# Streaming V past stationary softmax probabilities, with the row sum as a 65th column, in an attention-plus-experts kernel

## The chip, the cores and the metric

The kernel runs on one NeuronCore of a Trainium2 chip. The metric is the device time of the whole program in microseconds (us). Most figures are medians. A ratio is the mean time of one kernel's fast runs over the mean of the fast runs of the kernel before in the same rounds, so it isn't quite the ratio of the medians that stand beside it. Below, PE is TensorE, PEld its weight loads, DVE is VectorE, ACT is ScalarE.

## The reference, cut to what matters

Four batches of eight heads, 768 positions, head size 64. Three heads are full causal, five see a window of 64 and four sink positions. The attention result is the input of eight experts, weighted by a Sinkhorn-normalised router.

```python
scores = scale * np.matmul(q, k.transpose(0, 1, 3, 2))          # (4, 8, 768, 768)
scores = np.where(mask[None], scores, -1e9)
a = np.exp(scores - scores.max(-1, keepdims=True))
a = a / (a.sum(-1, keepdims=True) + 1e-9)
x = heads_side_by_side(np.matmul(a, v))                          # (3072, 512)
P = np.exp(x @ w_gate - (x @ w_gate).max())                      # router
for _ in range(8):
    P /= P.sum(1, keepdims=True) + 1e-9
    P /= P.sum(0, keepdims=True) + 1e-9
    P *= N / E
for e in range(8):
    out += P[:, e:e+1] * (np.maximum(x @ w1[e], 0) @ w2[e])
```

## The kernel before

Scores are computed transposed: keys on the partitions, 256 queries on the free axis. ACT takes the exponential into `PT`, DVE multiplies by masks. A unit (b, g, u) is 256 queries of four heads, done as two head pairs a = 0, 1. The product with V and the denominators are two sets of matmuls that stream the same `PT`:

```python
def gen_pv(b, g, u, a, PT, scale):
    if a == 0:
        accs[b, g, u] = [psA.tile([128, 512], F32, tag="pv", bufs=2, ...) for i in range(2)]
    pv, den = accs[b, g, u]
    for i, (kj, far, lo, hi, off) in enumerate(todo):
        cols = slice(256 * a + lo, 256 * a + hi)
        for hh in range(2):                      # two heads, on partitions 0-63 and 64-127
            nc.tensor.matmul(out=pv[64 * hh:64 * hh + 64, cols],
                             lhsT=(vf if far else vt)[:, h, kj, :],
                             rhs=PT[:, hh, off:off + hi - lo], ...)
        for hh in range(2):                      # row sums, 64 times over
            nc.tensor.matmul(out=den[64 * hh:64 * hh + 64, cols],
                             lhsT=onesf[:, h, min(kj, 1), :] if far else ones16,
                             rhs=PT[:, hh, off:off + hi - lo], ...)
        yield
    if a == 1:                                   # 1 / den as exp(-ln(den)), then one scaling
        nc.scalar.activation(out=rc, in_=den, func=AF.Ln, ...)
        nc.scalar.activation(out=rc, in_=rc, func=AF.Exp, scale=-1.0)
        scale.append(lambda: nc.vector.tensor_tensor(out=xT[u][:, :, c0:c0 + 256], in0=pv, in1=rc, op=ALU.mult))
```

Attention runs in 48 rounds. A round computes scores, their exponentials and masks, and in some rounds the products that have become ready. Between them PE gets "fillers": pieces of the first expert's layers for blocks of `x` that are finished (a layer-1 piece is one unit, a layer-2 piece two, 96 units in all). What is left runs between the Sinkhorn steps. In attention the kernel holds eight PSUM tiles of 128x512 f32, called banks here: four for scores, two for `pv` and `den`, two (tag `mo`) shared by fillers, preparing transposes of Q and K, and router logits.

The softmax here doesn't subtract the row's maximum and nothing guards it: scores larger than these inputs give would overflow.

## Time and profile before

| | us |
|---|---|
| median, 5 runs | 733.41 (732.26 to 733.88) |
| attention with fillers, to the first column-sum matmul | 184.8 |
| Sinkhorn loop with the rest of the fillers | 20.3 |
| experts 1 to 7 | 525 |

The busy time of each engine in these three stretches of the kernel before (columns: stretch, its length, then busy us and instruction counts by engine, granted PE clock, DMA share and GB/s):

```profile
core 0: us, PE busy (x) PEld busy (x) DVE busy (x) ACT busy (x) POOL busy (x), PEclk, DMA share, GB/s
0.00:184.80 184.80, 169.57 (x2258) 111.27 (x2258) 107.81 (x231) 126.95 (x180) 39.73 (x51) 1.00 0.74 78
184.80:205.10 20.30, 19.70 (x136) 13.01 (x137) 14.87 (x43) 9.18 (x16) 1.32 (x2) 1.00 0.12 20
205.10:730.00 524.90, 516.48 (x4682) 457.34 (x4681) 448.12 (x845) 292.47 (x600) 110.26 (x131) 1.00 0.57 97
```

PE looks 92% busy in attention (169.57 of 184.80 us), but the records of matmuls overlap: one of 256 columns lasts 273 ns, and the next pair starts after 109. As what a matmul takes from the array I count the distance to the next start. The timeline of PE before shows it (start, length, line, shape, count):

```profile
100.79 0.28 PE L296 MATMUL pv<-PT,vf 128*64 128x256 f16 x2
100.89 0.28 PE L303 MATMUL pv<-PT,onesf 128*64 128x256 f16 x2
101.00 0.28 PE L296 MATMUL pv<-PT,vf 128*64 128x256 f16 x2
101.11 0.28 PE L303 MATMUL pv<-PT,onesf 128*64 128x256 f16 x2
...
101.44 0.22 PE L296 MATMUL pv<-PT,v 128*64 128x128 f16 x2
101.50 0.22 PE L303 MATMUL pv<-PT,ones 128*64 128x128 f16 x1
```

A pair of 256-column matmuls, one head in each half of the array, takes 0.11 us and not 0.28; a pair of 128 columns takes 0.06. The rows alternate between product (L296) and denominator (L303): half of this time goes into row sums.

For every matmul I took the distance to the next start, capped at the spacing that the trace shows where nothing waits: 216 ns at 512 columns, 109 at 256, 56 at 128, 25 at 8. (In the count the cap is the straight line through the first three, and never below 25 ns.) These "occupied" times sum to 142.4 of 184.8 us in attention, 37.8 us of it for product and denominator. The other 42.4 us are waits, switches of tile mode (89 to 96 ns where the records show one without a wait: after a 256-column matmul, for one, the next start comes after 205 ns in place of 109 where the mode changes from 128x128 to 64x128; 165 switches by program order), a slow start (512-column matmuls 427 ns apart in the first 5 us) and a few lost records. In the expert phase the same count gives 513.5 of 525 us, so nothing is to be had there.

The instructions behind the accumulation, from the groups of the attention stretch (busy us, mean ns, then idle time before them and its releaser):

```profile
L314 DVE TENSOR_TENSOR xT<-pv,rc 128x512 f16<-128x512 f32 x24 | 16.5, 689 | 6.8 <-ACT rc L312 6.7
L312 ACT ACTIVATE rc<-rc 128x512 f32<-128x512 f32 x24 | 15.2, 635 | 0.5
L311 ACT ACTIVATE rc<-pv 128x512 f32<-128x512 f32 x24 | 14.5, 604 | 10.5 <-PE pv L303 10.5
```

Ln and Exp cost ACT 29.7 us, and each unit's two accumulators stay taken until they and the scaling are done.

### The profile page before, as it was taken

The page shows a single profiled execution, that of the slowest core. Times are in us where ns is not written, and L with a number is a line of the kernel's source. Part 1 is how long each engine was busy: PE and PEld are TensorE (multiplying, and loading weights), DVE is VectorE, ACT ScalarE, POOL GpSimd, SP SyncE. Part 2 cuts the span into 40 slices and gives each one's busy share as a digit, 9 for nine tenths or more (in the row PEclk, how much of TensorE's full clock was granted, in tenths as well). Part 3 has the DMA queues.
Part 4 walks back from the last instruction along what each step waited for, and adds up shares of the span by engine and source line. Part 5 has one row for each costly group of instructions (what it writes and reads, how often), then busy time and mean ns, then how long its engine had stood idle before and what let it go on. Part 6 is the DMA issues. An engine that isn't in the chain of part 4 may idle for free.

```text
span 730.4 us, 17366 instructions
## 1 busy us (share of the span) xinstructions
PE 705.7 (97%) x7072; PEld 581.6 (80%) x7072; DVE 570.8 (78%) x1118; ACT 428.6 (59%) x795; POOL 151.3 (21%) x183
## 2 busy tenths in 40 slices
PE   7898999999999999999999999999999999999996
PEld 3566576766758888888888888888888888888884
DVE  5646565564788998888788888888889888977787
ACT  5666777777478555555555555555555555555550
POOL 6303131000001213121312131213121312121210
PEclk9999999999999999999999999999999999999999
DMA  9999575300063428742864386438743874345785
GB/s 178 180 165 74 58 58 47 31 2 2 1 116 57 75 45 135 113 82 48 138 110 79 52 136 111 76 57 132 114 74 59 123 124 73 59 71 107 149 157 126
DMA packets 84224, 65.62 MB, mean 90 GB/s; under 512 B 48304, under 2 KB 64688, under 8 KB 84144
## 3 DMA queue, kind: packets, MB, share of 16 engines
q0 software_dynamic: 74976, 57.17, 55.0%
q1 hardware_dynamic: 7536, 6.30, 3.8%
q8 instruction: 55, 0.90, 0.5%
q10 hardware_dynamic: 1632, 1.05, 0.5%
q14 instruction: 25, 0.20, 0.1%
HBM read 52.45 MB, written 6.29 MB: 80 GB/s over the span
## 4 chain that ended last, share of the span: by engine, by line
PE 67%; DVE 1%; issue 0%; ACT 0%; DVEq 0%
PE l1y L707 19%; PE l2y L776 19%; PE l2w L776 10%; PE l1w L707 10%; PE l2z L776 5%; PE l1z L707 5%; DVE acc L793 1%; DVE S L644 0%; ACT R L716 0%; DVEq L887 0%; ACT add L790 0%
## 5 line engine op out<-in xcount | busy, mean ns | idle before, releaser
L798 POOL DMA_DIRECT2D acc<-add x120 | 101.5, 845 | 381.6 <-ACT add L790 346.9
L716 ACT ACTIVATE R<-l1y 128x512 f32<-128x512 f32 x164 | 98.7, 602 | 127.8 <-PE l1y L707 92.8
L776 PEld LDWEIGHTS <-S 128*128 128x128 f16 x1344 | 131.1, 98 | 17.1 <-DVE S L644 1.2
L707 PEld LDWEIGHTS <-S 128*128 128x128 f16 x1312 | 128.3, 98 | 17.1 <-issue 2.1
L793 DVE SCALAR_TENSOR_TENSOR acc<-l2y,Pne,acc 128x256 f32<-128x256 f32 x256 | 111.2, 476 | 29.9 <-PE l2y L776 29.8
L776 PEld LDWEIGHTS <-hT 128*128 128x128 f16 x1008 | 98.6, 98 | 12.0 <-issue 0.6
L707 PEld LDWEIGHTS <-w 128*128 128x128 f16 x984 | 96.3, 98 | 11.9 <-issue 0.6
L707 PE MATMUL l1y<-T,S 128*128 128x256 f16 x656 | 98.4, 273 | 1.4 <-ACT R L716 1.4
L448 ACT ACTIVATE PT<-sc 128x1024 f16<-128x1024 f32 (+1 forms) x96 | 83.7, 920 | 26.4 <-PE sc L439 25.1
L776 PE MATMUL l2y<-T,S 128*128 128x256 f16 x672 | 87.1, 273 | 0.0
L790 ACT ACTIVATE add<-l2w,Pne 128x256 f32<-128x256 f32 x80 | 33.7, 473 | 66.1 <-PE l2w L776 62.3
L644 DVE TENSOR_TENSOR S<-hT 128x1024 f16<-128x1024 f16 x84 | 57.6, 685 | 17.0 <-ACT hT L746 14.6
L722 DVE CUSTOM_DVE_ANT_0 hT<-l1z,R 128x512 f16<-128x512 f32 x82 | 56.2, 685 | 7.4 <-ACT R L716 7.3
L722 DVE CUSTOM_DVE_ANT_0 hT<-l1w,R 128x512 f16<-128x512 f32 x82 | 56.1, 685 | 4.3 <-PE l1w L707 0.4
L722 DVE CUSTOM_DVE_ANT_0 hT<-l1y,R 128x512 f16<-128x512 f32 x82 | 55.7, 679 | 0.1
L346 PE MATMUL l<-xT,w 128*128 128x256 f16 x384 | 49.4, 273 | 3.2 <-DVE xT L314 1.4
L746 ACT ACTIVATE hT<-l1y 128x512 f16<-128x512 f32 x82 | 49.0, 597 | 4.2 <-PE l1y L707 2.8
L716 ACT ACTIVATE R<-l1w 128x512 f32<-128x512 f32 x82 | 49.4, 603 | 0.0
L707 PE MATMUL l1z<-xT,w 128*128 128x256 f16 x328 | 49.4, 273 | 0.0
L707 PE MATMUL l1w<-T,S 128*128 128x256 f16 x328 | 49.4, 273 | 0.0
L707 PE MATMUL l1w<-xT,S 128*128 128x256 f16 x328 | 49.4, 273 | 0.0
L707 PE MATMUL l1y<-T,w 128*128 128x256 f16 x328 | 49.2, 272 | 0.1
(104 smaller groups left out, 1111.6 us busy)
## 6 DMA issues: line engine op xcount, KB each, us to landing
acc<-add POOLq DMA_DIRECT2D x120, 256.0 KB, 3.3
w<-in_moe_w_dram POOLq DMA_DIRECT2D x16, 1024.0 KB, 10.7
out_dram<-acc SPq DMA_DIRECT2D x44, 128.0 KB, 2.8
k<-in_k_dram POOLq DMA_DIRECT2D x11, 256.0 KB, 5.6
q<-in_q_dram POOLq DMA_DIRECT2D x11, 256.0 KB, 7.0
v<-in_v_dram POOLq DMA_DIRECT2D x12, 192.0 KB, 8.0
acc<-in_v_dram POOLq DMA_DIRECT2D x3, 256.0 KB, 7.5
acc<-in_q_dram ACTq DMA_DIRECT2D x2, 256.0 KB, 5.3
```

What stands on the lines that cost most here:

```text
L346: nc.tensor.matmul(out=l1[:, ts(fb % 2, 256)], lhsT=w1[:, dc, ts(fb, 128)], rhs=xT[dc // 2][:, dc % 2, c0:c0 + 256], start=(dc == 0), stop ...
L448: nc.scalar.activation(out=PT[:, :, c0:c0 + width], in_=sc[:, :, 0:width], func=AF.Exp, bias=0.0, scale=SCALE,)
L644: nc.vector.tensor_tensor(out=out_, in0=a_, in1=b_, op=op)
L707: nc.tensor.matmul(out=banks[g, bank][:, f, :], lhsT=lefts1[e][k - 1][:, dc, ts(2 * g + f, 128)], rhs=rights1[c][k - 1][:, dc, :], start=( ...
L716: nc.scalar.activation(out=R[name], in_=banks[g, bank], func=AF.Copy, bias=0.0, scale=1.0)
L722: nc.vector._custom_dve(TENSOR_ADD_SAT, out=block(g, i, n), in0=banks[g, bank], in1=R[name], s0=65504.0, s1=0.0)
L746: nc.scalar.activation(out=block(g, 1, 0), in_=banks[g, "y"], func=AF.Relu, bias=0.0, scale=1.0)
L776: nc.tensor.matmul(out=banks[bank][q], lhsT=lefts2[e, c][k - 1][:, q, f, :], rhs=rights2[e][k - 1][:, f, :], start=(first and (final or q ...
L790: nc.scalar.activation(out=t[:, q, :], in_=banks[bank][q], func=AF.Copy, bias=0.0, scale=w)
L793: nc.vector.scalar_tensor_tensor(out=dst, in0=banks[bank][q], scalar=w, in1=dst, op0=ALU.mult, op1=ALU.add,)
L798: nc.gpsimd.dma_start(out=acc[c][:, i, n, :, :], in_=t, accum_op=ALU.add)
```

## The change

The operands of the product change places. `PT` becomes the stationary operand, 128 queries at a time, and V streams: 64 columns and a 65th of ones, whose result is the row sum. The result has queries on the partitions, so normalising is a division by a number per partition and head. Then PE transposes it back, and ACT stores it. The order around it is changed too: products in every round, fillers spread evenly, 29 units left for the end in place of 24, three of them ahead of the last transposes.

```diff
 def pv_of(g):
-    res = [(kj, 1, 0, 256, 256 * kj) for kj in range(2 * g - 1)]
-    ...
+    res = [(kj, kj < 2 * g - 1 + s, s, 256 * kj + 128 * s) for kj in range(2 * g + 1) for s in range(2)]
+    return res + [(2 * g + 1, 0, 1, 512 * g + 256)]
...
+    DV = D + 2
...
-            vts[b] = ap.tile([128, H, NC, D], F16, tag="v16", name=f"v16_{b}")
+            vts[b] = ap.tile([128, H, NC, DV], F16, tag="v16", name=f"v16_{b}")
+            nc.vector.memset(vts[b][:, :, :, D:DV], 1.0)
...
     def gen_pv(b, g, u, a, PT, scale):
+        pv = psA.tile([128, 2, 2, DV], F32, tag="pv", bufs=2, name=f"pv_{b}_{g}_{u}_{a}")
+        for i, (kj, far, sb, off) in enumerate(todo):
+            for hh in range(2):
+                nc.tensor.matmul(
+                    out=pv[:, sb, hh, 0:D + 1], lhsT=PT[:, hh, off:off + 128],
+                    rhs=(vf if far else vt)[:, 4 * u + 2 * a + hh, kj, 0:D + 1], ...)
+            yield
+        def normalize():
+            nc.vector.reciprocal(out=rc, in_=pv[:, :, :, D])
+            nc.vector.tensor_tensor(out=xn[:, a], in0=pv[:, :, :, 0:D],
+                in1=rc.unsqueeze(3).broadcast_to([128, 2, 2, D]), op=ALU.mult)
+            if a == 1:
+                turns.append((b, g, u))
+    def turn():
+            xt = psA.tile([128, 512], F32, tag="mo", bufs=2, name=f"xt_{b}_{g}_{u}").bitcast(F16)
+            # four 128x128 transposes of xn into xt
+            nc.scalar.activation(out=xT[u][:, :, c0:c0 + 256], in_=xt[:, 0:512]..., func=AF.Copy)
+            # then the block's fillers are queued
...
-    with_sums = (0, 1, 3, 5, 7, 9, 11)
-    quota = {0: 2, 1: 2, 2: 4, 4: 4, 6: 4, 8: 4, 10: 4}
+    quotas = [0] * 4 + [1] * (rounds - 4)
-            fill(-(quotas[n] * (24 - left[0]) // sum(quotas[n:])))
+            fill(-(quotas[n] * (29 - left[0]) // sum(quotas[n:])))
...
+    late[0] = True
     finish_sums()
+    fill(3)
+    turn()
     emit_logits(B - 1)
-    late[0] = True
```

More of the change, by code (lines that the diff above doesn't have):

```diff
@@ L28, in pv_of @@
 def pv_of(g):
-    res = [(kj, 1, 0, 256, 256 * kj) for kj in range(2 * g - 1)]
-    if g:
-        kj = 2 * g - 1
-        res += [(kj, 0, 0, 128, 256 * kj), (kj, 1, 128, 256, 256 * kj + 128)]
-    return res + [(2 * g, 0, 0, 256, 512 * g), (2 * g + 1, 0, 128, 256, 512 * g + 256)]
+    res = [(kj, kj < 2 * g - 1 + s, s, 256 * kj + 128 * s) for kj in range(2 * g + 1) for s in range(2)]
+    return res + [(2 * g + 1, 0, 1, 512 * g + 256)]
 PTW = 1408
@@ L128, in place_v @@
         nc.scalar.activation(
-            out=v_tile(0)[:, :, 2 * g:2 * g + 2, :].rearrange("p h n d -> p n h d"),
+            out=v_tile(0)[:, :, 2 * g:2 * g + 2, 0:D].rearrange("p h n d -> p n h d"),
             in_=t.rearrange("p n (h d) -> p n h d", h=H), func=AF.Copy, bias=0.0, scale=1.0,
@@ L135, in load_v_heads @@
             nc.gpsimd.dma_start(
-                out=v_tile(b)[64 * o:64 * o + 64, h0:h1].rearrange("p h n d -> p (h n) d"),
+                out=v_tile(b)[64 * o:64 * o + 64, h0:h1, :, 0:D].rearrange("p h n d -> p (h n) d"),
                 in_=v[b, h0:h1].rearrange("h (n p c) d -> c p (h n) d", p=64, c=2)[o],
@@ L207 @@
                             op0=ALU.mult, op1=ALU.add)
-    ones16 = constp.tile([128, D], F16, tag="ones16")
-    nc.vector.memset(ones16, 1.0)
     sinks = [slice(64 * o, 64 * o + (n_sink + 1 - o) // 2) for o in range(2)]
@@ L213 @@
     farf = cp.tile([128, H, 2], F16, tag="farf")
-    onesf = cp.tile([128, H, 2, D], F16, tag="onesf")
     def make_keep():
@@ L237, in make_far @@
             nc.vector.memset(farf[rows, :, 0], 1.0)
-    def make_far_ones():
-        nc.scalar.activation(out=onesf, in_=farf.unsqueeze(3).broadcast_to([128, H, 2, D]),
-                             func=AF.Copy, bias=0.0, scale=1.0)
     wg16 = constp.tile([128, 4, E], F16, tag="wg16")
@@ L269, in emit_vfar @@
         if b not in vfs:
-            vfs[b] = ap.tile([128, H, 4, D], F16, tag="vf", bufs=1, name=f"vf_{b}")
+            vfs[b] = ap.tile([128, H, 4, DV], F16, tag="vf", bufs=1, name=f"vf_{b}")
         for n in (2 * g - 2, 2 * g - 1):
@@ L273, in emit_vfar @@
                 out=vfs[b][:, :, n, :], in0=vts[b][:, :, n, :],
-                in1=farf[:, :, min(n, 1)].unsqueeze(2).broadcast_to([128, H, D]), op=ALU.mult,
+                in1=farf[:, :, min(n, 1)].unsqueeze(2).broadcast_to([128, H, DV]), op=ALU.mult,
             )
@@ L280, in keep_warm @@
             nc.tensor.matmul(out=t[:, 0:src.shape[1]], lhsT=lhsT, rhs=src, start=True, stop=True)
-    accs = {}
+    xns, turns = {}, []
     def gen_pv(b, g, u, a, PT, scale):
-        if a == 0:
-            accs[b, g, u] = [psA.tile([128, 512], F32, tag="pv", bufs=2, name=f"pv_{b}_{g}_{u}_{i}")
-                             for i in range(2)]
-        pv, den = accs[b, g, u]
+        pv = psA.tile([128, 2, 2, DV], F32, tag="pv", bufs=2, name=f"pv_{b}_{g}_{u}_{a}")
         vt, vf = vts[b], vfs.get(b)
@@ L290, in gen_pv @@
         todo = pv_of(g)
-        for i, (kj, far, lo, hi, off) in enumerate(todo):
-            cols = slice(256 * a + lo, 256 * a + hi)
-            first, last = i == 0, i == len(todo) - 1
+        for i, (kj, far, sb, off) in enumerate(todo):
             for hh in range(2):
-                h = 4 * u + 2 * a + hh
                 nc.tensor.matmul(
-                    out=pv[64 * hh:64 * hh + 64, cols],
-                    lhsT=(vf if far else vt)[:, h, kj, :],
-                    rhs=PT[:, hh, off:off + hi - lo], start=first, stop=last,
-                )
-            for hh in range(2):
-                h = 4 * u + 2 * a + hh
-                nc.tensor.matmul(
-                    out=den[64 * hh:64 * hh + 64, cols],
-                    lhsT=onesf[:, h, min(kj, 1), :] if far else ones16,
-                    rhs=PT[:, hh, off:off + hi - lo], start=first, stop=last,
+                    out=pv[:, sb, hh, 0:D + 1], lhsT=PT[:, hh, off:off + 128],
+                    rhs=(vf if far else vt)[:, 4 * u + 2 * a + hh, kj, 0:D + 1],
+                    start=(i == 0 and hh == 0), stop=(i == len(todo) - 1 and hh == 1),
+                    skip_group_check=True,
@@ L307, in gen_pv @@
                 )
             yield
-        if a == 1:
-            rc = ap.tile([128, 512], F32, tag="rc", name=f"rc_{b}_{g}_{u}")
-            nc.scalar.activation(out=rc, in_=den, func=AF.Ln, bias=0.0, scale=1.0)
-            nc.scalar.activation(out=rc, in_=rc, func=AF.Exp, bias=0.0, scale=-1.0)
-            c0 = b * S + 256 * g
-            scale.append(lambda: nc.vector.tensor_tensor(
-                out=xT[u][:, :, c0:c0 + 256], in0=pv.rearrange("p (a c) -> p a c", a=2),
-                in1=rc.rearrange("p (a c) -> p a c", a=2), op=ALU.mult))
-            yield
+        if a == 0:
+            xns[b, g, u] = ap.tile([128, 2, 2, 2, D], F16, tag="xn", name=f"xn_{b}_{g}_{u}")
@@ new lines, in gen_pv @@
+        xn = xns[b, g, u]
+        def normalize():
+            rc = ap.tile([128, 2, 2], F32, tag="rc", bufs=4, name=f"rc_{b}_{g}_{u}_{a}")
+            nc.vector.reciprocal(out=rc, in_=pv[:, :, :, D])
+            nc.vector.tensor_tensor(
+                out=xn[:, a], in0=pv[:, :, :, 0:D],
+                in1=rc.unsqueeze(3).broadcast_to([128, 2, 2, D]), op=ALU.mult)
+            if a == 1:
+                turns.append((b, g, u))
+        scale.append(normalize)
+    def turn():
+        while turns:
+            b, g, u = turns.pop(0)
+            xn = xns.pop((b, g, u))
+            xt = psA.tile([128, 512], F32, tag="mo", bufs=2, name=f"xt_{b}_{g}_{u}").bitcast(F16)
+            for a in range(2):
+                for sb in range(2):
+                    nc.tensor.transpose(out=xt[:, ts(2 * a + sb, 128)], in_=xn[:, a, sb],
+                                        identity=ident16)
+            c0 = b * S + 256 * g
+            nc.scalar.activation(
+                out=xT[u][:, :, c0:c0 + 256], in_=xt[:, 0:512].rearrange("p (a c) -> p a c", a=2),
+                func=AF.Copy, bias=0.0, scale=1.0)
+            if u == 1:
+                one, two = first_steps(b, g)
+                at = 4 if (b, g) == (0, 1) else len(fillers)
+                fillers[at:at] = one
+                fillers.extend(two)
@@ L480, in finish_sums @@
             del sums_of[i, a]
-            b, g, u = units[i]
             held += scale
-            if not hold:
-                for f in scale:
-                    f()
-            if (u, a) == (1, 1):
-                one, two = first_steps(b, g)
-                at = 4 if (b, g) == (0, 1) else len(fillers)
-                fillers[at:at] = one
-                fillers.extend(two)
-        return held
-    with_sums = (0, 1, 3, 5, 7, 9, 11)
-    quota = {0: 2, 1: 2, 2: 4, 4: 4, 6: 4, 8: 4, 10: 4}
+        if not hold:
+            for f in held:
+                f()
+        return held
     rounds = len(tasks) // 2
-    quotas = [quota.get(n % 12, 0) if n >= 6 else 0 for n in range(rounds)]
-    quotas[4:6] = [2, 2]
+    quotas = [0] * 4 + [1] * (rounds - 4)
     def spend(n):
         if quotas[n]:
-            fill(-(quotas[n] * (24 - left[0]) // sum(quotas[n:])))
+            fill(-(quotas[n] * (29 - left[0]) // sum(quotas[n:])))
     def sum_later(n):
@@ L541 @@
         soften(r1, (0,))
-        make_far_ones()
         sum_later(0)
@@ L548 @@
         emit_prep(*preps.pop())
-        scale[0]()
+        for f in scale:
+            f()
         warm(4)
@@ L553 @@
         soften(r2, (0,))
+        turn()
         scale = finish_sums(True)
         soften(r2, (1,))
-        scale[0]()
+        for f in scale:
+            f()
         sum_later(2)
@@ L560 @@
         soften(scores(3))
+        warm(3)
         place_v(1)
+        turn()
         finish_sums()
@@ L565 @@
         soften(scores(4))
+        turn()
         finish_sums()
@@ L569 @@
         soften(scores(5))
+        turn()
         finish_sums()
@@ L575 @@
         soften(scores(n))
-        if n % 12 in with_sums:
-            if n == 7:
-                place_v(2)
-            if preps:
-                emit_prep(*preps.pop())
-            finish_sums()
+        if n == 7:
+            place_v(2)
+        if preps:
+            emit_prep(*preps.pop())
+        turn()
+        finish_sums()
         sum_later(n)
@@ L585 @@
         spend(n)
+    late[0] = True
     finish_sums()
+    fill(3)
+    turn()
     emit_logits(B - 1)
-    late[0] = True
     rs = xp.tile([128, NB], F32, tag="rs")
```

## The prediction

> **What bounds it now.** The table of busy time by stretches shows three phases: attention with interleaved first-expert work to 182.6 us, the Sinkhorn loop to 205 us, then 525 us of expert products. The change touches only the first two. In 45 to 182.6 us PE is busy 130.5 of 137.6 us, ACT 96.7, DVE 80.2. PE's busy time counts pipeline latency, so I take start-to-start spacing from the timeline instead. Probability-times-V and denominator matmuls run as pairs in two 64-column halves: a pair of 256 columns every 0.109 us, a pair of 128 every 0.056. Counted over all attention, PE's array is occupied about 141 of 182.6 us; about 15 us of the rest are switches between tile modes (95 ns each, 165 of them), the remainder waits. So PE's in-order stream bounds attention, ACT next.
>
> **Removed from PE.** 896 matmuls (224 pairs x 109 ns + 224 x 56 ns) = about 37 us.
>
> **Added to PE.** 672 full-array matmuls with the probabilities stationary and 65 columns of V streaming, the 65th being the row sum. The router's 24 matmuls (128x128 weights, 8 columns) start every 25 ns, and 256-column matmuls start every 109 ns with their loads hidden. So I expect about 30 ns each[...]. Total 20 us. Then 96 transposes at 56 ns, 5.4 us. Tile-mode switches fall from 165 to 150, -1.4 us. [...] Net about -13 us, nearly all on PE's stream.
>
> **ACT.** Out: 24 Ln (0.60) and 24 Exp (0.63), 29.6 us, and the 1.07 us ones-mask. In: 24 evacuations at 0.6, 14.4 us. Net -16 us, off the bound.
>
> **DVE.** Out: 24 scalings of 0.69, 16.5 us. In: 48 reciprocals (0.2) and 48 half-size scalings (0.42), about 30 us. Net +13 us.
>
> **Moves.** Fillers spread over all rounds and five more units (0.87 us each) are left for after the last product: that moves 4.3 us of PE work, it saves none. They cover the last normalisation, where PE now waits 1.8 us. The transposed result takes one of two PSUM banks shared with fillers and preparation: I charge 3 us of new waits.
>
> **Sum.** 733.4 - 13 - 1.5 + 3 = about 721.5 us. Range 713 to 730. Chances: faster by over 2% 0.30, within 2% 0.65, slower 0.05.
>
> **What would show it.** Right: the new product's matmuls start 30 ns apart; attention (start to the first column-sum matmul) shorter by 6 to 12 us although the Sinkhorn phase grows 2 to 4 us; the expert phase unchanged at 525 us; ACT's Ln/Exp gone, DVE's total up about 13 us. Wrong: spacing of 50 ns or more (loads not hidden behind 65 columns), which would cancel the gain; or attention shortened by much less than PE's saving, with PE waiting for ACT's exponentials, DVE's masks or the shared bank.
>
> **What would make it wrong.** The shared bank serialising preparation, transposes and fillers; DVE in order, its normalisation queued behind masks; start-up being bound by DMA and exponentials, so its PE saving is worth nothing. In the other direction: before, both accumulators belong to one unit until Ln, Exp and scaling end; freed banks could remove several microseconds of waits and pass 2%.

The sum: its terms as written make 721.9, put as about 721.5 us. The 30 ns at 65 columns, and with them the 20 us, stand as an estimate: the straight line through the recorded 56 ns at 128 columns and 109 at 256 gives 30. The 0.2 and 0.42 us for DVE were estimates of mine; the trace after has 174 and 423 ns. "In order" is what the trace of the kernel before shows: by source line, its 1118 DVE and 795 ACT records start in the order of the built program, and 7055 of the program's 7064 matmuls do.

## The result, and the profile after

The changed kernel takes 718.67 us (median of 9 runs), against 732.15 for the kernel before in the same rounds. The ratio is 0.9808, with a 95% interval of 0.9798 to 0.9818: 13.5 us faster. The interval lies on both sides of 2%, so whether it is faster by over 2% stays undecided. The prediction had 721.5, within 713 to 730.

One of the nine executions took 1428.6 us, and it was the profiled one. Its page shows PE busy for 99% of the span and 256-column matmuls of 444 ns in place of 273: from beginning to end the wide matmuls ran at half the rate (start to start 222 ns at 256 columns, 443 at 512, both medians; at 65 columns the median is 34). Its trace holds no clock record at all, and its mean clock of 1.0 is only the value for want of one. The other eight runs of the same program lie between 717.6 and 719.1 us. I ran it again for a usable profile (718.67 us, profiled at 716.6) and use nothing of the slow one.

The three stretches after, in the usable profile:

```profile
0.00:169.60 169.60, 154.78 (x2116) 100.77 (x2117) 114.10 (x305) 110.99 (x153) 39.82 (x51) 0.99 0.84 85
169.60:190.70 21.10, 21.10 (x155) 14.66 (x154) 14.56 (x42) 10.16 (x17) 0.76 (x1) 1.00 0.08 12
190.70:716.00 525.30, 516.87 (x4681) 457.32 (x4681) 448.96 (x845) 293.03 (x601) 110.74 (x131) 1.00 0.56 97
```

Attention is 15.2 us shorter, the Sinkhorn loop 0.8 us longer, and the experts are unchanged. ACT lost 16 us of work in attention.

The new product in the timeline of PE after:

```profile
114.18 0.40 PE L312 MATMUL xt<-ident,xn 128*128 128x128 f16 x4
114.41 0.28 PE L283 MATMUL pv<-vf,PT 128*128 128x65 f16 x4
114.53 0.22 PE L283 MATMUL pv<-v,PT 128*128 128x65 f16 x2
114.60 0.22 PE L283 MATMUL pv<-vf,PT 128*128 128x65 f16 x2
114.66 0.35 PE L283 MATMUL pv<-v,PT 128*128 128x65 f16 x6
114.84 1.03 PE L351 MATMUL l<-xT,w 128*128 128x256 f16 x8
```

The 14 matmuls from 114.41 to 114.84 take 0.43 us, 30 ns each, though each has its own load of a 128x128 stationary operand (672 loads, whose records last 97 ns each). The same amount of attention (g = 1, one head pair) took before two pairs of 256 columns and three of 128, twice: 2 x (2 x 0.109 + 3 x 0.056), 0.77 us. The four transposes take 0.23 us, 57 ns each.

What follows the accumulation, from the groups of the attention stretch after:

```profile
L297 DVE TENSOR_TENSOR xn<-pv,rc 128x256 f16<-128x256 f32 x48 | 19.9, 423 | 1.0
L315 ACT ACTIVATE xT<-xt 128x512 f16<-128x512 f16 x24 | 14.6, 606 | 3.7 <-PE xt L312 3.6
L296 DVE RECIPROCAL rc<-pv 128x4 f32<-128x4 f32 x48 | 7.9, 174 | 2.0 <-PE pv L283 2.0
```

ACT does one evacuation of 606 ns where it did Ln and Exp. DVE does 48 x (174 + 423) ns, 28.7 us, where it did 16.5.

The account of PE, worked out from the starts in each trace as above, for all kernels. "Rest" is the length minus what is occupied: waits, switches, stretches of half clock and lost records.

| kernel | median us | attention | occupied | rest |
|---|---|---|---|---|
| before | 732.1 to 732.7 | 184.8 | 142.4 | 42.4 |
| changed | 718.67 | 169.6 | 128.2 | 41.4 |
| new_product_old_order | 722.80 | 174.8 | 129.9 | 44.9 |
| old_product_new_order | 730.42 | 181.3 | 140.2 | 41.1 |
| no_tail | 722.73 | 175.3 | 129.8 | 45.5 |
| stream128 | 730.39 | 181.7 | 145.8 | 35.9 |
| no_den (wrong) | 721.92 | 174.3 | 129.5 | 44.8 |
| act_load | 724.08 | 175.5 | 128.3 | 47.2 |
| act_load2 | 723.31 | 173.7 | 128.4 | 45.3 |
| dve_load | 722.83 | 173.8 | 128.5 | 45.3 |
| full_prep | 716.90 | 167.7 | 127.9 | 39.8 |
| xt_in_pv | 714.22 | 165.5 | 128.3 | 37.2 |
| full_prep_xt_in_pv | 711.76 | 162.9 | 128.0 | 34.9 |

One execution's rest is good to about 2 us only. For four runs the trace kept is another execution than the one read here: after_again (span 716.8 us, rest 41.2), new_product_old_order (721.7, rest 46.3), old_product_new_order (728.8, rest 41.5) and stream128 (730.5, rest 37.8). Their occupied times agree with the table to 0.1 us. The start-up differs from one execution to the next: the mean granted clock over the first 15 us was 1.00 in the kernel before (whose clock record begins at 13.4 us only) and 0.89 in after_again, over the first 55 us 0.97 in act_load2 and 0.94 in act_load.

In attention the array's work fell by 14.2 us, of which 1.8 us are fillers moved into the Sinkhorn loop; product and denominators went from 37.8 to 19.7 us, the new transposes take 5.3. Waits and switches together hardly moved, by -1.0 us. The work explains the result, but the unchanged rest could hide a gain and a loss. The experiments ask that.

### The profile page after: what moved, and what is told of

It is laid out like the page before. It is cut to its first block, busy times and chain, and to the rows that moved or that the text cites. A ratio compares the mean times of both kernels' runs of the same rounds, so it can differ in the third digit from the quotient of the medians.

```text
span 1426.9 us, 17118 instructions
## 1 busy us (share of the span) xinstructions
PE 1415.8 (99%) x6947; PEld 863.4 (61%) x6947; DVE 606.1 (42%) x1192; ACT 439.6 (31%) x771; POOL 151.2 (11%) x183
## 4 chain that ended last, share of the span: by engine, by line
PE 99%; DMA 0%; ACT 0%; DVE 0%; issue 0%; SPq 0%
PE l2y L780 22%; PE l1y L711 21%; PE l2w L780 11%; PE l1w L711 11%; PE l L365 6%; PE l L351 6%; PE l2z L780 6%; PE l1z L711 5%; PE sc L444 3%; PE pv L283 3%; PE tr L248 2%; PE l1b L691 1%; PE warm L272 1%; PE xt L312 1%; DMA acc<-in_k_dram 0%; PE lgp L332 0%
## 5 line engine op out<-in xcount | busy, mean ns | idle before, releaser
L780 PEld LDWEIGHTS <-S 128*128 128x128 f16 x1344 | 199.8, 149 | 114.2 <-DVE S L648 0.2
L711 PEld LDWEIGHTS <-S 128*128 128x128 f16 x1312 | 195.0, 149 | 111.3
L780 PEld LDWEIGHTS <-hT 128*128 128x128 f16 x1008 | 149.3, 148 | 85.9
L711 PEld LDWEIGHTS <-w 128*128 128x128 f16 x984 | 146.4, 149 | 84.1 <-issue 0.7
L711 PE MATMUL l1y<-T,S 128*128 128x256 f16 x656 | 187.8, 444 | 0.0
L780 PE MATMUL l2y<-T,S 128*128 128x256 f16 x672 | 174.6, 445 | 0.0
L351 PE MATMUL l<-xT,w 128*128 128x256 f16 x384 | 94.9, 441 | 0.7 <-ACT xT L315 0.4
L711 PE MATMUL l1y<-xT,w 128*128 128x256 f16 x328 | 93.9, 444 | 0.0
L365 PE MATMUL l<-w,hT 128*128 128x512 f16 x192 | 93.4, 677 | 0.0
L780 PE MATMUL l2z<-w,hT 128*128 128x256 f16 x336 | 87.9, 443 | 0.0
L780 PE MATMUL l2y<-T,hT 128*128 128x256 f16 x336 | 87.5, 444 | 0.0
## 6 DMA issues: line engine op xcount, KB each, us to landing
w<-in_moe_w_dram POOLq DMA_DIRECT2D x16, 1024.0 KB, 10.2
out_dram<-acc SPq DMA_DIRECT2D x44, 128.0 KB, 2.4
```

What stands on the lines that cost most here:

```text
L351: nc.tensor.matmul(out=l1[:, ts(fb % 2, 256)], lhsT=w1[:, dc, ts(fb, 128)], rhs=xT[dc // 2][:, dc % 2, c0:c0 + 256], start=(dc == 0), stop ...
L365: nc.tensor.matmul(out=l2, lhsT=hT[fc // 2][:, o:o + 128], rhs=w2[:, fc, :], start=(fc == 0), stop=(fc == 7),)
L711: nc.tensor.matmul(out=banks[g, bank][:, f, :], lhsT=lefts1[e][k - 1][:, dc, ts(2 * g + f, 128)], rhs=rights1[c][k - 1][:, dc, :], start=( ...
L780: nc.tensor.matmul(out=banks[bank][q], lhsT=lefts2[e, c][k - 1][:, q, f, :], rhs=rights2[e][k - 1][:, f, :], start=(first and (final or q ...
```

## The experiments

Theory A: PE's stream bounds attention, and a shorter stream pays. Rival B: the gain comes from relieving ACT and the accumulators. Rival C: it comes from the new order of products and fillers. All three parts changed at once, so none can be read off the two traces alone.

A caution for all of them: from the seventh round on the order on each engine is left to a scheduler. An edit also moves some of PE's instructions; a comparison of the built programs showed me one to two in a hundred in other places. Differences below about 1 us are therefore not interpreted.

### after_again: the changed kernel once more

No edit.

> The changed kernel once more, because its first profile fell into an execution [...] (1427 us). All theories: 718 to 719 us, and a profile comparable with that of before. Theory A (PE's stream got shorter): new product's matmuls start 30 ns apart, PE's array is occupied about 13 us less before the Sinkhorn loop's end, waits about unchanged. Rival B (waits went away because Ln, Exp and the shared accumulators went, and PE's saving is mostly lost again): PE's spacing is over 45 ns, and the sum of its waits is smaller by 8 us or more. Rival C (the new order of fillers does it): waits smaller, and the next two runs tell.

718.67 us, ratio 0.9818 (0.9796 to 0.9840). Spacing 30 ns, occupied time 14.2 us less in attention, rest about equal. This is as theory A has it. B's clause of slow loads is out.

### new_product_old_order and old_product_new_order: the two halves

```diff
 # new_product_old_order, from the changed kernel:
-    quotas = [0] * 4 + [1] * (rounds - 4)
+    quotas, with_sums = (those of before)
-            fill(-(quotas[n] * (29 - left[0]) // sum(quotas[n:])))
+            fill(-(quotas[n] * (24 - left[0]) // sum(quotas[n:])))
+        if n % 12 in with_sums:                  # prep, turn, finish_sums only here
-    fill(3)                                      # and late[0] = True after emit_logits
 # old_product_new_order: the reverse edits on the kernel before
```

> The changed product, normalisation and transposes, but fillers and products in the rounds and amounts of before (24 units left for the Sinkhorn loop, products only in the rounds that had them, no filler ahead of the last transposes). Theory A and B: most of the gain stays, 719 to 723 us. Rival C: most of it goes, 728 to 733 us.

> The kernel before with only the new rounds: products in every round, fillers evenly spread, 29 units left and three of them ahead of the last logits. Theory A and B: 729 to 733 us, a gain of at most 3 us. Rival C: 719 to 724 us.

| | old order | new order |
|---|---|---|
| old product | 732.46 | 730.42 |
| new product | 722.80 | 718.67 |

The new product alone is worth 9.7 us, the order alone 2.0, both 13.8. Rival C falls as the main cause. But the order is worth 4.1 us with the new product, which is 30% of the gain.

### no_tail: which part of the order?

```diff
-            fill(-(quotas[n] * (29 - left[0]) // sum(quotas[n:])))
+            fill(-(quotas[n] * (24 - left[0]) // sum(quotas[n:])))
...
-    late[0] = True
     finish_sums()
-    fill(3)
     turn()
     emit_logits(B - 1)
+    late[0] = True
```

> The changed kernel with its even fillers, but without what it does at the end of attention: 24 units left in place of 29, none ahead of the last transposes. The order was worth 4.1 us with the new product (722.8 against 718.7). If the covered tail is the cause: 721 to 723 us, with PE idle some 2 us longer between the last product and the first column sum. If the even spread over the rounds is the cause: 718 to 719.5 us.

722.73 us: all of the 4.1 us are gone, and what remains equals the old order (722.80). The even spread is worth nothing that shows. (The line with `late` is undone too: it moves the Relu of the last fillers from DVE to ACT.) The timelines say why. First the end of attention in this run, without weight loads (in brackets: idle time before, and what ended it):

```profile
168.85 0.36 PE L283 MATMUL pv<-v,PT 128*128 128x65 f16 x6 [0.29 <-DVE PT L465]
169.24 0.18 DVE L296 RECIPROCAL rc<-pv 128x4 f32<-128x4 f32 x1 [0.45 <-PE pv L283]
169.46 0.42 DVE L297 TENSOR_TENSOR xn<-pv,rc 128x256 f16<-128x256 f32 x1
169.94 0.29 PE L312 MATMUL xt<-ident,xn 128*128 128x128 f16 x2 [0.74 <-DVE xn L297]
170.26 0.60 ACT L315 ACTIVATE xT<-xt 128x512 f16<-128x512 f16 x1 [2.06 <-PE xt L312]
170.91 0.32 PE L332 MATMUL lgp<-wg,xT 128*128 128x8 f16 x6 [0.69 <-ACT xT L315]
171.09 4.34 PE L351 MATMUL l<-xT,w 128*128 128x256 f16 x24
```

The same in the changed kernel:

```profile
164.21 0.35 PE L283 MATMUL pv<-v,PT 128*128 128x65 f16 x6
164.40 1.24 PE L365 MATMUL l<-w,hT 128*128 128x512 f16 x5
164.60 0.18 DVE L296 RECIPROCAL rc<-pv 128x4 f32<-128x4 f32 x1 [0.47 <-PE pv L283]
164.81 0.42 DVE L297 TENSOR_TENSOR xn<-pv,rc 128x256 f16<-128x256 f32 x1
165.47 0.39 PE L312 MATMUL xt<-ident,xn 128*128 128x128 f16 x4
165.68 0.60 ACT L369 ACTIVATE acc<-l 128x512 f32<-128x512 f32 x1 [1.31 <-PE l L365]
166.17 0.59 ACT L315 ACTIVATE xT<-xt 128x512 f16<-128x512 f16 x1
166.32 0.80 PE L332 MATMUL lgp<-wg,xT 128*128 128x8 f16 x24 [0.46 <-ACT acc L369]
166.98 1.89 PE L365 MATMUL l<-w,hT 128*128 128x512 f16 x8
```

The last block has a chain of reciprocal, scaling, transposes, evacuation and logits, and nothing else is ready. Without the kept fillers PE waits 0.74 and 0.69 us in it. With them PE computes while DVE works. The larger part is another. The 24 layer-1 matmuls at 171.09 last 4.34 us, where 24 at 109 ns would take 2.6, and they wait for nothing: most of them start 213 ns apart. The clock column of two neighbouring stretches of 3.4 us in this run shows why:

```profile
167.50:170.90 3.40, 1.70 (x36) 1.27 (x36) 1.46 (x4) 1.30 (x2) 0.00 (x0) 1.00 0.00 0
170.90:174.30 3.40, 3.39 (x22) 2.46 (x23) 1.51 (x4) 0.81 (x2) 0.00 (x0) 0.50 0.00 0
```

The stretches at the same place in the changed kernel:

```profile
163.00:166.40 3.40, 2.94 (x32) 1.66 (x31) 1.32 (x4) 1.86 (x4) 0.00 (x0) 1.00 0.00 0
166.40:169.80 3.40, 3.40 (x43) 2.37 (x43) 1.51 (x4) 1.19 (x4) 0.00 (x0) 1.00 0.00 0
```

After the 3.4 us in which PE was busy for only half (1.70 us), the granted clock was 0.50 for the next 3.4 us; after those with 86% (2.94 us) it stayed at 1.00. In no_tail about 15 matmuls ran at 213 in place of 109 ns, 1.6 us lost. new_product_old_order has the same drop at the same place (0.51 from 170.7 to 174.1 us, after a stretch of 3.4 us with PE 59% busy). The granted clocks of whole executions agree: seven of the twelve fast ones of the changed kernel have 0.997 or 0.998, while none of the eight of these two runs is above 0.995. The kernel before, whose end has PE busy for 2.57 of 3.40 us, shows no drop there (1.00). (Where such a stretch is laid is my choice, so these shares are rough. And that the idle half brings the slow clock about is my reading: the traces show that one follows the other.) Its longest wait of PE and of DVE at that place:

```profile
181.54 0.69 DVE L314 TENSOR_TENSOR xT<-pv,rc 128x512 f16<-128x512 f32 x1 [1.90 <-ACT rc L312]
182.33 0.38 PE L346 MATMUL l<-xT,w 128*128 128x256 f16 x2 [0.69 <-ACT hT L351]
```

But the busy share alone doesn't decide it. In the kept trace of old_product_new_order a stretch with PE busy for 51% is followed by full clock:

```profile
103.37:106.78 3.41, 1.75 (x23) 1.20 (x24) 3.41 (x8) 2.41 (x4) 3.41 (x5) 1.00 1.34 131
106.78:110.20 3.42, 3.08 (x45) 2.56 (x43) 3.04 (x7) 1.23 (x2) 0.65 (x1) 1.00 2.35 159
```

The occupied share may separate the cases better. By its timeline, the array in no_tail was occupied for 31% of the stretch ahead of the drop (1.04 of 3.40 us); in the changed kernel, at the same place, for 78% (2.64). The trace of the kernel before has full clock from 13.4 to 726.8 us of the span and 0.50 after that. In 209 equal pieces of 3.413 us, the first 208 were occupied for 52% or more and followed by full clock; the last, at the end of the program, was occupied for 25% (PE busy for 30%) and followed by 0.50. These are few cases, and I make no rule of them.

So of the 4.1 us, plain waits are 1.0 (0.74 + 0.69, less the 0.46 that the changed kernel keeps), the half clock is 1.6, and the remaining 1.5 us I did not trace. (The expectation had some 2 us of idle PE; the waits are half of that.)

### stream128: what is a microsecond of PE worth?

```diff
-        pv = psA.tile([128, 2, 2, DV], F32, tag="pv", ...)
+        pv = psA.tile([128, 2, 2, 2 * D], F32, tag="pv", ...)
...
-                    out=pv[:, sb, hh, 0:D + 1], lhsT=...,
-                    rhs=(vf if far else vt)[:, 4 * u + 2 * a + hh, kj, 0:D + 1],
+                    out=pv[:, sb, hh, :], lhsT=...,
+                    rhs=twice((vf if far else vt)[:, 4 * u + 2 * a + hh, kj, 0:D]),  # 128 columns
...
-            nc.vector.reciprocal(out=rc, in_=pv[:, :, :, D])
+            nc.vector.reciprocal(out=rc, in_=pv[:, :, :, 2 * D - 1])
```

> The changed kernel, but each of the 672 product matmuls streams 128 columns in place of 65 (V's row read twice, shifted by two, so that the last column is still the row sum; results stay right). Spacing [...] goes from 30 to 56 ns, 17.6 us more on PE. Theory A: 733 to 737 us, the gain is gone although nothing else changes. Rival B or C: 718 to 724 us, since PE's array time was not what the gain came from.

730.39 us, results right. The attention stretch of this run:

```profile
0.00:181.70 181.70, 170.88 (x2116) 116.73 (x2117) 114.93 (x305) 111.41 (x153) 39.66 (x51) 1.00 0.81 80
```

Occupied time rose by 17.6 us, as computed (the 14 product matmuls from 125.14 to 125.94 us start 57 ns apart, where 30 ns were before), and ACT and DVE did the same work as in the changed kernel. The time rose by 11.7 us, so a microsecond of array time was worth 0.66 us. The rest fell from 41.4 to 35.9 (from 41.2 to 37.8 in the kept traces): by the times, a third of the added work fitted into waits. My expectation of 733 to 737 missed this way. It also means that of the saving of the change, a part turned into waits. Rivals B and C, which expected at most 724, fall.

### no_den: the same price, measured from the other side

```diff
-            for hh in range(2):
+            for hh in range(2 if i == 0 else 0):     # denominators: first key block only
                 nc.tensor.matmul(out=den[64 * hh:64 * hh + 64, cols], ...,
-                    start=first, stop=last)
+                    start=True, stop=True)
```

> The kernel before with only the first denominator matmul of each product; the others are left out, so results are wrong on purpose. That takes 13.6 us of array time off PE (18.8 us less 48 pairs at 0.109 us) and nothing off ACT or DVE. If PE's time is paid in full: 719 us. At the price that stream128 showed (11.7 us for 17.6): about 723 us. If ACT and the latency of Ln and Exp bound attention (rival B): 730 us or more.

721.92 us; the results are wrong. 10.2 us for 13.6 us of array time is 0.75; the trace counts 12.9 us (142.4 to 129.5), which makes it 0.79. Leaving the denominators out of the old product, with the work of ACT and DVE, the number of accumulators and the order as they were, gives about what the new product gives under the old order. Theory A stands. One thing did shift: Ln can now start before the product is done, and from a unit's last product matmul to the end of its scaling it is 1.71 us on average, in place of 1.94.

No run frees the accumulators alone. An estimate from stream128 says what they, ACT and DVE can be worth together. That run keeps everything of the change but the array time: 166.1 us of it to the end of the Sinkhorn loop, against 160.9 before. At its own price of 0.66 it would take about 727 us with equal array time, 5.5 us less than the kernel before. The order is worth 2.0 to 4.1 of that, which leaves a net 1 to 4 us for ACT's relief and the accumulators (rival B), less the added DVE work.

### act_load and act_load2: is ACT's relief a part?

```diff
             nc.scalar.activation(out=xT[u][:, :, c0:c0 + 256], in_=xt..., func=AF.Copy)
+            for i in range(2):
+                idle = ap.tile([128, 512], F32, tag="idle", bufs=1, ...)
+                nc.scalar.activation(out=idle, in_=ident16[:, 0:1].broadcast_to([128, 512]), func=AF.Copy)
 # act_load2: in_=xT[u][:, :, c0:c0 + 256], the result just written
```

> The changed kernel with two idle 512-column writes on ACT per unit (1.2 us), behind the evacuation of the transposes, so about as much ACT work as Ln and Exp were (28.8 us in all), on no chain of data. Theory A (PE's array time pays, ACT is off the bound): 718.5 to 722 us. Rival B (the gain came from relieving ACT by 16 us): 727 us or more.

724.08 us, between the two expectations, and the run was not what I meant: the idle writes read nothing late, and the scheduler pulled them all into the first two batches (all 48 run before 93 us; by summed durations ACT has 47.0 us of work from 0 to 55 us and 46.4 from 55 to 100, in place of 36.5 and 31.7 in the kept trace of the changed kernel). So I mended it.

> The last ACT run again, mended: in it the scheduler had moved the idle writes of all units into the first two batches (ACT busy 48 and 47 us there, unchanged in the last two), since they read nothing that was late. Now they read the result just written, so each runs behind its own evacuation; 28.8 us of ACT work evenly spread. If ACT is off the bound: 719 to 722 us. If relieving ACT of 16 us was a main part of the gain (at least half of each us paid): 730 us or more.

723.31 us, again above what A allowed. The attention stretch shows ACT's load back above that of the kernel before, 137 against 127 us:

```profile
0.00:173.70 173.70, 156.19 (x2117) 100.95 (x2118) 114.88 (x305) 137.05 (x201) 39.70 (x51) 0.99 0.83 83
```

The 48 writes took 630 ns each, 30.2 us, and cost 4.6: 0.15 us per microsecond. ACT is not quite off the bound, but its relief is a small part. At this price the 16 us that the change took off ACT are worth some 2.5 us, an estimate.

### dve_load: what did the new DVE work cost?

```diff
                 in1=rc.unsqueeze(3).broadcast_to([128, 2, 2, D]), op=ALU.mult)
+            idle = ap.tile([128, 2, 2, D], F16, tag="idle", bufs=1, ...)
+            nc.vector.tensor_tensor(out=idle, in0=xn[:, a],
+                in1=rc.unsqueeze(3).broadcast_to([128, 2, 2, D]), op=ALU.mult)
```

> The changed kernel with one idle DVE multiplication of 256 columns behind each of the 48 normalisations, some 0.3 to 0.42 us each, 15 to 20 us in all, more than the 12 us that the change added to DVE. If DVE is off the bound: 718.5 to 721 us. If the change's DVE work is paid by half or more: 726 us or more, and the gain was that much smaller than PE's saving for this reason.

722.83 us, between the two. 48 x 417 ns are 20 us, and they cost 4.2: 0.21 per microsecond. By the same kind of estimate the 12 us that the change added to DVE cost some 2.5 us, which cancels what ACT gave. Neither engine carries the result.

### full_prep: one tile mode less

The preparing transposes of Q and K still ran as pairs in 64-column halves. With two heads side by side in memory, one whole-array transpose does a pair's work (57 ns to the next start in the changed kernel's trace, as against 56 for a pair).

```diff
-                ap.tile([128, H, 2, D], F16, tag=n, bufs=3, ...)
+                ap.tile([128, 2, H, D], F16, tag=n, bufs=3, ...)
...
-                    for hh in range(2):
-                        nc.tensor.transpose(out=tr[64 * hh:64 * hh + 64, ts(4 * i + 2 * a + c, 128)],
-                                            in_=src[:, 4 * u + 2 * a + hh, c, :], identity=ident16)
+                    nc.tensor.transpose(out=tr[:, ts(4 * i + 2 * a + c, 128)],
+                                        in_=src[:, c, h:h + 2, :].rearrange("p h d -> p (h d)"), identity=ident16)
 # and each load of Q or K is two, one per parity of the position
```

> A try to beat both: K and Q are kept with two heads side by side, so that the preparing transposes use the whole array (192 in place of 384, no 64-column mode), as the new product does. Tile-mode switches fall from 150 to 125, 2.4 us at 95 ns. At the price of stream128 that is 716.5 to 717.5 us. Against it: K and Q arrive in 256-byte pieces and twice as many DMAs, which can cost more in the first 60 us, where the DMA engines are at 90% or more: then 719 us or more.

716.90 us, ratio 0.9786 (0.9764 to 0.9807), 1.8 us under the changed kernel. Array work is the same (127.9), the rest is 1.6 us smaller, near the 2.4 us of 25 switches at 95 ns. The feared cost of smaller pieces of Q and K does not show.

A first version, which kept the old layout and gave the transpose two separate runs of 64 columns as its stationary operand, did not build.

### xt_in_pv and full_prep_xt_in_pv: were the shared banks a cost?

```diff
-        pv = psA.tile([128, 2, 2, DV], F32, tag="pv", bufs=2, ...)
+        pv = psA.tile([128, 512], F32, tag="pv", bufs=2, ...)[:, 0:4 * DV].rearrange("p (s h d) -> p s h d", s=2, h=2)
...
-            xt = psA.tile([128, 512], F32, tag="mo", bufs=2, ...).bitcast(F16)
+            xt = psA.tile([128, 512], F32, tag="pv", bufs=2, ...).bitcast(F16)
```

> The changed kernel with the transposed result in one of the two banks of the products, in place of the two shared with fillers and preparation. The prediction charged 3 us for waits on the shared banks. If that charge was right: 715.5 to 717.5 us. If the shared banks cost nothing: 718 to 719.5 us. Slower than 720 us would say only that the products need both of their banks.

> The faster kernel found so far (716.9 us, whole-array preparation) with the same move of the transposed result. The same differences as in the run before it: 714 to 716 us if the shared banks cost, 716 to 718 us if not.

714.22 us, ratio 0.9749 (0.9734 to 0.9765), and 711.76 us, ratio 0.9711 (0.9692 to 0.9731). Both are below even the range expected for a costly shared bank, and both beat the changed kernel clearly. The attention stretch of xt_in_pv:

```profile
0.00:165.50 165.50, 154.07 (x2116) 99.72 (x2116) 112.99 (x305) 110.90 (x153) 39.70 (x51) 0.99 0.91 88
```

Same work on all engines, 4.1 us shorter, all of it out of the rest. The waits have moved. In the changed kernel PE waited on ACT's evacuation `xT` with fillers, logits and a warm-up matmul (waits of PE in attention: total us, times, longest):

```profile
PE l L351 <- ACT xT L315: 2.0, 4, 0.9
...
PE warm L272 <- ACT xT L315: 0.9, 1, 0.9
...
PE lgp L332 <- ACT xT L315: 0.6, 3, 0.2
```

In xt_in_pv these are gone from the longest, and the products wait for the same evacuation:

```profile
PE pv L284 <- ACT xT L316: 2.6, 3, 1.6
```

The bank that the transposed result takes is held until ACT has evacuated it. In the kept trace of the changed kernel that starts 0.8 us after the last transpose on average, and in 14 of 24 cases two exponentials run in between. In the shared pair this stops whatever comes next there; in the products' pair it stops the next product, which comes later. This last sentence is how I read it. That moving the result to another bank is worth 4.4 us is shown, give or take the scheduler's other moves: tile-mode switches fell by 5 as well, some 0.5 us. In the other direction, the profile of this run has one stretch of half clock, from 23.2 to 26.6 us, after PE had been half busy in the start-up (1.71 of 3.40 us).

## Why the prediction was right, point by point

- **The mechanism held.** 37 us out and 20 us in on PE were predicted; the trace has 37.8 and 19.7. The transposes were to take 5.4 us and take 5.3; tile-mode switches were to fall from 165 to 150, and did. The spacing of 65-column matmuls is 30 ns, while the record of a load of `PT` lasts 97, so the loads are hidden. Array time over the whole program fell by 12.4 us (142.4 + 18.5 + 513.5 in the three stretches before, 128.2 + 20.3 + 513.5 after).
- **The step "nearly all on PE's stream" was too strong.** PE's time was worth 0.66 to 0.79 per microsecond, by stream128 and no_den. The rest grew when work left: under the old order by 2.5 us (42.4 to 44.9), of which about 1.6 are the half clock at the end.
- **The 3 us for the shared banks were of the right kind and somewhat small.** Moving one tile gave 4.4 us back. The name of the cost was right beforehand, and a kernel 4.4 us faster was one edit away.
- **The mis-sized term of the sum is the end of attention.** "They cover the last normalisation, where PE now waits 1.8 us", with 1.5 us in the sum, was worth 4.1 us. I had counted waits alone, and misjudged those: in the trace of the kernel before, PE's longest wait there is 0.69 us; a wait of 1.90 us is DVE's. The new product's end in no_tail leaves PE half busy for 3.4 us, and the half clock that followed more than doubled the cost of the waits (1.6 us on top of 1.0). With the old product the order gave 2.0 us; its profile has a half-clock stretch of its own, at 59.9 to 63.3 us (mean clock 0.50), so that this is no clean measure of the cover.
- **"Attention shorter by 6 to 12 us although the Sinkhorn phase grows 2 to 4 us" was wrong.** It was 15.2 and 0.8. I counted five moved units, but the kept units that run ahead of the first column sum still lie in the attention stretch: array time in the loop grew by 1.8 us, two units. The prediction also ended the phase at 182.6 us; the first column-sum matmul starts at 184.8.
- **The other engines.** ACT's -16 us is met in its stretch (127.0 to 111.0). DVE's +13 us is about met by the sum of durations (+11.7 us in the kept traces); busy time, where overlapping neighbours count once, rose by 6.8 us over the program.
- **Errors cancelled in part:** a price of 1 where it is about 0.7, against an end of attention that was worth 2.6 us more. That 721.5 came within 3 us of the measured time is in part luck. The 9.7 us of the product alone are 0.77 of the 12.5 us of array time that it removed, between the two prices. But the prices are slopes, each from one edit, and that run also holds the uncovered end, 25 fewer switches and the changes on ACT and DVE; I did not find a sum of all these that explains the 9.7 us to better than a few microseconds. That remainder stays open.

## What to carry to other kernels

When one operand of an accumulation is narrow, compare what streams in either arrangement: here streaming 65 columns of V, with the sum as one of them, replaced streaming 128 or 256 columns of probabilities twice, and the extra weight loads cost nothing that shows (30 ns from one 65-column matmul to the next, each with its load). After such a change look at the new chain's last instance and at the banks that it shares, for those were worth about 4 us each, against a gain of 13.5. Keep PE fed through such a chain: in no_tail a stretch of 3.4 us with PE busy for half was followed by 3.4 us at a granted clock of 0.50, 1.6 us on top of 1.0 us of waits. And measure the price of an engine's time by adding work that does nothing, before counting on a saving.
